# Turning q, k and the exponentials by transposing transfers instead of on TensorE

## The chip, the cores and the metric

The kernel runs on one core of one Trainium2 chip. The metric is the device time of one execution in microseconds. In the profile PE is TensorE (matmuls), PEld its weight loads, DVE is VectorE, ACT is ScalarE, POOL is GpSimd (here it issues loads), SP is SyncE (here it issues transfers within SBUF, and stores).

## The reference

Attention with a few global tokens, then a two-layer network over all tokens:

```python
batch, n_heads, seq_l, seq_g, head_dim = (8, 8, 512, 32, 64)      # window = 32
out_g = matmul(softmax(q_g @ [k_g, k_l].T * scale), [v_g, v_l])   # 32 global queries see all 544 keys
s_ll = where(|pos_q - pos_k| <= 32, q_l @ k_l.T * scale, -1e9)    # 512 local queries see a band
out_l = matmul(softmax([q_l @ k_g.T * scale, s_ll]), [v_g, v_l])  # and the 32 global keys
x = concat([out_g, out_l]).transpose(0, 2, 1, 3).reshape(4352, 512)
h = x @ w_in                                                      # 512 -> 2048
out = (h * clip(h + 3, 0, 6) / 6) @ w_out                         # 2048 -> 512, float32
```

## The kernel before

Work is cut into operations, each with an engine, a length, the operations it depends on, the buffer that it takes and those that it gives back, and a key (when it should come). `Plan.lay` (from line 98) lays them out ahead of time: at each step it takes the operation that can start first, by lengths and latencies written into the kernel, and of those that start within 40 ns the one with the lowest key. For transfers it keeps a small model of two queues, POOL's and SP's (`Transfers`, line 27). The result is a fixed order for every engine and queue; on the chip each engine goes through its order and waits for semaphores where its next instruction isn't ready. Attention of a batch is meant to run `AHEAD` keys (line 470) before the network of that batch; a batch's network is 4 keys long. Where PE would be idle before batch 2, filler matmuls on a tile of zeros are put in (line 944).

For each batch b of 8:

- Loads (POOL, line 380): four tiles of 128 rows of q and k go to `nat` (4 buffers, float16, q and k side by side: 128 x 2 x 512), v to `ve`. q and k of the global tokens go to `natg`.
- `turn_qk` (line 547): eight matmuls with the identity (line 556) turn one `nat` tile, 128x128 each, into the PSUM tile `t`, of which there is one; one copy on ACT or DVE (lines 284, 286) moves it to `qk`, where the head's 64 dimensions lie on partitions and the rows along the free side. `turn_g` (line 568) does the same for the global rows. `qk` has two buffers, by b % 2.
- Strips: from batch 1 on, seven transfers on SP's queue (line 519) put copies of `ve` into `st` so that each 32 queries find their 96 local rows of v and the 32 global ones on 128 partitions.
- `local_step` (line 595), four times per batch: scores `s` of 128 queries for 8 heads (lines 614, 621, 628), then for each head the masked smallest value of the negated scores (DVE, line 640) and the exponential with its sum (ACT, line 651), then the division by the sum into `pn` (two DVE instructions, line 665, four heads each). Eight matmuls with the identity (line 672) turn `pn` (128 queries x 8 heads x 128 keys) into `t`; a copy moves it to `et`. The product with the strips (`av`, lines 690 and 695) goes to `a`, and two copies put it into `xt`, the network's input.
- `global_steps` (line 720) does the 32 global queries, with turnings of its own (line 766) and the product at line 780.
- `moe_local` (line 842): the first layer (line 802) in 16 groups of four 128x512 matmuls, a relu on ACT (line 809) and the combining product on DVE (line 813) into `gs`; the second layer (line 824) in 16 groups of four, for four tiles of 128 rows; a copy to `ot` and a store on SP's queue (line 839). After all batches `moe_global` does the same for the 256 global rows.

`pn` and `et` have two buffers each (lines 257 and 258), `sm`, which feeds `pn`, has two, and `t` is shared by all turnings.

Of the kernel before, what the change touches and what calls it, by code (L numbers as in the profile page):

```python
# [9 lines left out]
FP16 = mybir.dt.float16  # L10
# [63 lines left out]
class Plan:  # L74
# [5 lines left out]
    AHEAD, WAIT = 0.3, 0.0  # L80
# [7 lines left out]
    def add(self, eng, dur, emit, deps=(), key=0.0, acq=None, rel=(), dma=None):  # L88

        o = Op(eng, dur, emit, deps, key, acq, rel, 0, dma)  # L90
        o.can = {eng: dur} if isinstance(eng, str) else dict(zip(eng, dur))
        o.n = len(self.ops)
        self.ops.append(o)
        for r in rel:
            r.held += 1
        return o
# [101 lines left out]
def kernel(  # L198
# [12 lines left out]
    nc = tc.nc  # L211
    P = 128

    B, H, Sl, D = q_l.shape
# [3 lines left out]
    NP = H // 2  # L218
    NJ = Sl // P
    NDFF = dff // P  # L220
    G = Sg
    UQ = 32
    NU = P // UQ
    KL = 3 * UQ
    KC = Sl + 2 * UQ
# [14 lines left out]
    def many(n, shape, dtype, name, pool=sb):  # L240
        return [pool.tile(shape, dtype, tag=f"{name}{i}", name=f"{name}{i}") for i in range(n)]

    NS, NX = 2, 3
    psS = many(1, [P, 2, 512], FP32, "s", pp)
    psT = many(1, [P, 1024], FP16, "t", pp)
    psA = many(1, [P, 2, 512], FP32, "a", pp)
    psM = many(3, [P, 512], FP32, "m", pp)

    nat = many(4, [P, 2, HD], FP16, "nat")
    natg = many(2, [P, HD], FP16, "natg")  # L250
    gt = many(2, [P, NP, P], FP16, "gt")
    kgz = many(2, [P, NP, 2, G], FP16, "kgz")
    qk = many(2, [P, NP, 2, KC], FP16, "qk")
    ve = many(2, [P, NV, HD], FP16, "ve")
    st = many(2, [P, NJ * NU, HD], FP16, "st")
    sm = many(NS, [P, H, P], FP32, "sm")
    pn = many(NS, [P, H, P], FP16, "pn")
    et = many(2, [P, H, P], FP16, "et")
    sg = many(2, [P, S], FP32, "sg")
    pg = many(2, [P, NV * P], FP16, "pg")  # L260
    eg = many(1, [P, 2, NV, P], FP16, "eg")
# [16 lines left out]
    add = plan.add  # L278
# [3 lines left out]
    def copy(op, out, in_):  # L282
        if op.eng == "ACT":
            nc.scalar.copy(out=out, in_=in_)  # L284
        else:
            nc.vector.tensor_copy(out=out, in_=in_)  # L286
# [65 lines left out]
    def clear():  # L352
        for r in range(2):
            for p in range(NP):
                nc.vector.memset(qk[r][:, p, 1, 0:UQ], 0.0)
                nc.vector.memset(qk[r][:, p, 1, KC - UQ:KC], 0.0)
            nc.vector.memset(ve[r][:, NJ, :], 0.0)
        nc.vector.memset(kgz[1], 0.0)

# [67 lines left out]
    def turn_first(na, lq, lk, nh, lh):  # L427

        def pe_q(op):
            ps = psM[op.slot].bitcast(FP16)  # L430
            for p in range(NP):
                nc.tensor.matmul(out=ps[:, p * P:(p + 1) * P], lhsT=nat[na.slot][:, 0, p * P:(p + 1) * P],
                                 rhs=ident, is_transpose=True)
        tq = add("PE", 225, pe_q, [na, lq, prep["ident"]], key=-5.5, acq="M", rel=[na])

        def ev_q(op):
            copy(op, qk[0][:, :, 0, UQ:UQ + P], psM[tq.slot].bitcast(FP16)[:, 0:NP * P].rearrange(
                "d (p s) -> d p s", p=NP))
        q = add(BOTH, (450, 300), ev_q, [tq, prep["clear"]], key=-7.5, rel=[tq])
        w = P + UQ  # L440

        def pe_k(op):
            ps = psM[op.slot].bitcast(FP16)
            for p in range(NP):
                nc.tensor.matmul(out=ps[:, p * w:p * w + P], lhsT=nat[na.slot][:, 1, p * P:(p + 1) * P],
                                 rhs=ident, is_transpose=True)
                nc.tensor.matmul(out=ps[:, p * w + P:(p + 1) * w],
                                 lhsT=pn[nh.slot].rearrange("s h d -> s (h d)")[0:UQ, p * P:(p + 1) * P],
                                 rhs=ident[0:UQ, 0:UQ], is_transpose=True)
        tk = add("PE", 350, pe_k, [na, lk, lh, prep["ident"]], key=-5.5, acq="M", rel=[na, nh])  # L450

        def ev_k(op):
            copy(op, qk[0][:, :, 1, UQ:UQ + w], psM[tk.slot].bitcast(FP16)[:, 0:NP * w].rearrange(
                "d (p s) -> d p s", p=NP))
        return q, add(BOTH, (540, 380), ev_k, [tk, prep["clear"]], key=-7.5, rel=[tk])

# [10 lines left out]
        return o  # L467

    gav = {}
    TIGHT, AHEAD, KEPT, PART, W_OUT = 2, 6.0, 1, {0: 128, 1: 256}, -5.5  # L470
    BLOCKS = ((0, 1), (2, 3))
    SPREAD = 0

# [70 lines left out]

    def turn_qk(b, j, ld, key, which=(0, 1)):
        r = b % 2
        w0, n = which[0], len(which)

        def pe(op):
            ps = psT[op.slot]
            for i in which:
                for p in range(NP):
                    c0 = ((i - w0) * NP + p) * P
                    nc.tensor.matmul(out=ps[:, c0:c0 + P], lhsT=nat[ld[0].slot][:, i, p * P:(p + 1) * P],  # L556
                                     rhs=ident, is_transpose=True)
        t = add("PE", 225 * n, pe, [*ld, prep["ident"]], key=key, acq="T", rel=ld[:1])

        def ev(op):  # L560
            copy(op, qk[r][:, :, w0:w0 + n, UQ + j * P:UQ + (j + 1) * P],
                 psT[t.slot][:, 0:n * NP * P].rearrange("d (i p s) -> d p i s", i=n, p=NP))
        deps = [t, prep["clear"]]
        if b >= 2:
            deps += [S_op[b - 2, jj] for jj in range(max(j - 1, 0), min(j + 1, NJ - 1) + 1)] + gS_op[b - 2]
        return add(BOTH, (450 * n, 300 * n), ev, deps, key=key - 2, rel=[t])

    def turn_g(b, ld, key, after=()):
# [26 lines left out]
    def local_step(b, j, key):  # L595
# [9 lines left out]
        def pe(op):  # L605
            ps = psS[op.slot]
            if kept:
                for p in range(NP):
                    for u in range(NU):
                        q0 = UQ + j * P + u * UQ  # L610
                        for lo, n, at in pieces(u) + [(None, G, place_g(u))]:
                            for e in range(2):
                                rows = slice(e * D, (e + 1) * D)
                                nc.tensor.matmul(out=ps[u * UQ:(u + 1) * UQ, e, p * P + at:p * P + at + n],
                                                 lhsT=qk[r][rows, p, 0, q0:q0 + UQ],
                                                 rhs=gt[g][rows, p, kg0:kg0 + G] if lo is None
                                                 else qk[r][rows, p, 1, q0 - UQ + lo:q0 - UQ + lo + n])
                return
            for p in range(NP):
                for e in range(2):  # L620
                    nc.tensor.matmul(out=ps[:, e, p * P:p * P + G],
                                     lhsT=qk[r][:, p, 0, UQ + j * P:UQ + (j + 1) * P], rhs=kgz[r][:, p, e, :])
            for p in range(NP):
                for u in range(NU):
                    for e in range(2):
                        rows = slice(e * D, (e + 1) * D)
                        q0 = UQ + j * P + u * UQ
                        nc.tensor.matmul(out=ps[u * UQ:(u + 1) * UQ, e, p * P + G:(p + 1) * P],  # L628
                                         lhsT=qk[r][rows, p, 0, q0:q0 + UQ],
                                         rhs=qk[r][rows, p, 1, q0 - UQ:q0 + 2 * UQ])  # L630
        s = add("PE", 900 if kept else 600, pe, [qkT[b, j], keyT[b, j], keyT[b, 0 if b == j == 0 else min(j + 1, NJ - 1)], kg[b]], key=key, acq="S")
        S_op[b, j] = s
        first = None
# [36 lines left out]
        def tr(op):  # L670
            for h in range(H):
                nc.tensor.matmul(out=psT[op.slot][:, h * P:(h + 1) * P], lhsT=pn[pn_op.slot][:, h, :],  # L672
                                 rhs=ident, is_transpose=True)
        t = add("PE", 450, tr, scs, key=key - 0.2, acq="T", rel=[pn_op])
        et_op = add("DVE", 0, lambda op: None, [t], key=key - 0.3, acq="et")

        def ev(op):
            copy(op, et[et_op.slot].rearrange("k h q -> k (h q)"), psT[t.slot])
        e_ = add(BOTH, (900, 600), ev, [et_op], key=key - 2, rel=[t])

        tight = b < TIGHT

# [37 lines left out]
    def global_steps(b, key):  # L720
# [5 lines left out]
        for e in range(2):  # L726
            rows = slice(e * D, (e + 1) * D)

            def pe(op, rows=rows):
                ps = psS[op.slot].rearrange("q a c -> q (a c)")  # L730
                for p in range(NP):
                    nc.tensor.matmul(out=ps[p * G:(p + 1) * G, 512 - G:512], lhsT=gt[g][rows, p, g0:g0 + G],
                                     rhs=gt[g][rows, p, g0 + G:g0 + 2 * G])
                for p in range(NP):
                    nc.tensor.matmul(out=ps[p * G:(p + 1) * G, 512:1024], lhsT=gt[g][rows, p, g0:g0 + G],
                                     rhs=qk[r][rows, p, 1, UQ:UQ + Sl])
            s = add("PE", 360, pe, [gT[b // 2]] + [keyT[b, j] for j in range(NJ)], key=key + 0.2 * e, acq="S")
            gS_op[b].append(s)
            so = add("DVE", 0, lambda op: None, [s], key=key, acq="stat")
# [32 lines left out]
            def ev(op, e=e, t=t):  # L772
                copy(op, eg[eg_op.slot][:, e].rearrange("k i q -> k (i q)"), psT[t.slot][:, 0:NV * P])
# [208 lines left out]
```

## Time and profile before

| | |
|---|---|
| median of 3 runs | 356.17 us (355.71 to 357.87) |
| the profiled execution | 355.24 us |
| its span, first to last instruction | 353.5 us |
| its granted TensorE clock, mean | 0.995 |
| turning q and k (L556), matmuls | 248, 31 groups of 8 |
| turning exponentials (L672), matmuls | 256, 32 groups of 8 |
| copies of 128x1024 out of `t`, to `qk` | 18 on DVE (683 ns), 13 on ACT (1021 ns) |
| the same to `et` | 18 on DVE (687 ns), 14 on ACT (1009 ns) |

Times on an engine are those of the profiled execution. The mean time of one matmul is longer than what it takes of PE, since matmuls follow each other in a pipeline; what a group takes is read from its start to the start of the next group.

### The profile page before, as it was taken

Reading aid. Unit: us, or ns where it says so; the run is one execution under the profiler, and the core shown is the slowest. Engines: PE = TensorE matmul, PEld = TensorE weight load, DVE = VectorE, ACT = ScalarE, POOL = GpSimd, SP = SyncE. Lnnn points to the kernel's source line nnn. Section 1 sums busy time; section 2 is a strip of 40 time slices with the busy share of each in tenths; the row PEclk is TensorE's granted clock in tenths of the full one; section 3 lists DMA queues with packets and bytes.
Section 4 is the critical chain, followed back from the end, with each engine's and each line's share of the span. In section 5 each row is a group of like instructions: output and inputs, shape, how many; then the busy total and the mean of one; then the engine's idle time right before and its main releaser. Section 6 shows DMA issues by size and latency. Waiting matters only on the chain.

```text
span 353.5 us, 11319 instructions
## 1 busy us (share of the span) xinstructions
PE 339.5 (96%) x4414; PEld 204.0 (58%) x4414; DVE 279.5 (79%) x1004; ACT 258.8 (73%) x792; POOL 106.2 (30%) x139
## 2 busy tenths in 40 slices
PE   7977979999999999999999999999999999999995
PEld 3565877667965555555555555555465544445642
DVE  6999978989996999888998899886997794076300
ACT  3898859759885999587987799859976893275411
POOL 8929712931680514151525123500000000000000
PEclk9999989999999999999999999999999999999999
DMA  9999999999999999599998999795001100200012
GB/s 158 174 195 131 172 253 164 138 189 259 91 149 240 168 219 103 37 154 179 166 64 123 193 159 70 68 212 146 0 32 41 53 2 0 91 30 1 32 51 98
DMA packets 123093, 42.47 MB, mean 120 GB/s; under 512 B 108320, under 2 KB 116000, under 8 KB 123040
## 3 DMA queue, kind: packets, MB, share of 16 engines
q0 software_dynamic: 106560, 17.05, 65.2%
q1 hardware_dynamic: 16480, 24.71, 24.9%
q8 instruction: 34, 0.56, 0.6%
q14 instruction: 19, 0.16, 0.1%
HBM read 35.19 MB, written 8.91 MB: 125 GB/s over the span
## 4 chain that ended last, share of the span: by engine, by line
PE 56%; DVE 20%; DMA 11%; POOL 7%; issue 3%; ACT 1%; SPq 0%; POOLq 0%; ACTq 0%
PE m L824 27%; PE m L802 18%; DVE gs L813 7%; DMA wout<-in_moe_w_out_dram 6%; DVE sm L640 4%; DMA win<-in_moe_w_in_dram 3%; POOL ve L380 3%; DVE pn L665 3%; POOL nat L380 2%; PE a L695 2%; PE t L672 2%; PE t L556 2%; PE s L628 2%; DVE xt L286 1%; DMA ve<-in_v_l_dram 1%
## 5 line engine op out<-in xcount | busy, mean ns | idle before, releaser
L824 PE MATMUL m<-wout,gs 128*128 128x512 f16 x544 | 130.3, 379 | 0.1
L802 PE MATMUL m<-xt,win 128*128 128x512 f16 (+2 forms) x768 | 124.7, 312 | 0.7 <-DVE gs L813 0.6
L813 DVE SCALAR_TENSOR_TENSOR gs<-t,m 128x512 f16<-128x512 f32 x136 | 91.2, 681 | 30.3 <-ACT t L809 29.7
L651 ACT ACTIVATE sm<-sm,stat 128x128 f32<-128x128 f32 x256 | 100.0, 394 | 16.1 <-DVE stat L640 15.7
L809 ACT ACTIVATE t<-m 128x512 f32<-128x512 f32 x136 | 81.1, 599 | 25.5 <-PE m L802 24.2
L802 PEld LDWEIGHTS <-win 128*128 128x128 f16 x832 | 70.1, 100 | 47.0 <-issue 5.3
L824 PEld LDWEIGHTS <-gs 128*128 128x128 f16 x544 | 49.7, 98 | 49.7 <-issue 1.0
L640 DVE CUSTOM_DVE_ANT_0 sm<-s,mask 128x128 f32<-128x128 f32 x256 | 59.8, 283 | 5.3 <-PE s L628 4.6
L651 ACT ACTIVATION_READ_ACCUMULATOR sm<-sm,stat 128x1 f32 x256 | 49.1, 192 | 0.0
L380 POOL DMA_DIRECT2D nat<-in_q_l_dram x30 | 27.1, 902 | 67.2 <-PE t L556 60.8
L665 DVE TENSOR_TENSOR pn<-sm,stat 128x512 f16<-128x512 f32 x64 | 43.9, 686 | 0.7
L284 ACT COPY ot<-m 128x512 f32<-128x512 f32 x24 | 14.1, 586 | 28.8 <-PE m L824 25.9
L380 POOL DMA_DIRECT2D ve<-in_v_l_dram x40 | 32.1, 821 | 0.2
L380 POOL DMA_DIRECT2D nat<-in_k_l_dram x30 | 27.2, 907 | 4.3 <-DVE stat L640 3.0
L284 ACT CAST xt<-a 64x512 f16<-64x512 f32 (+1 forms) x35 | 20.2, 577 | 7.1 <-PE a L695 4.7
L640 DVE DVE_READ_ACCUMULATOR2_ANT stat<- 128x1 f32 x256 | 21.1, 83 | 0.0
L672 PEld LDWEIGHTS <-pn 128*128 128x128 f16 x256 | 16.7, 98 | 6.7 <-issue 0.7
L556 PE MATMUL t<-ident,nat 128*128 128x128 f16 x248 | 19.1, 219 | 1.2 <-DVE qk L286 0.9
L556 PEld LDWEIGHTS <-nat 128*128 128x128 f16 x248 | 15.9, 98 | 6.9 <-issue 2.1
L672 PE MATMUL t<-ident,pn 128*128 128x128 f16 x256 | 19.7, 219 | 0.1
L944 PE MATMUL a<-idle 128*128 128x512 f16 x54 | 16.0, 420 | 3.6 <-DVE xt L286 1.8
L695 PEld LDWEIGHTS <-st 128*128 128x128 f16 x384 | 14.1, 98 | 4.2
(81 smaller groups left out, 318.3 us busy)
## 6 DMA issues: line engine op xcount, KB each, us to landing
out_dram<-ot SPq DMA_DIRECT2D x32, 256.0 KB, 3.5
st<-ve SPq DMA_DIRECT2D x14, 384.0 KB, 5.3
nat<-in_q_l_dram POOLq DMA_DIRECT2D x30, 128.0 KB, 4.8
nat<-in_k_l_dram POOLq DMA_DIRECT2D x30, 128.0 KB, 5.3
st<-ve SPq DMA_DIRECT2D x7, 512.0 KB, 7.1
st<-ve SPq DMA_DIRECT2D x14, 256.0 KB, 6.1
ve<-in_v_l_dram POOLq DMA_DIRECT2D x24, 128.0 KB, 5.5
win<-in_moe_w_in_dram POOLq DMA_DIRECT2D x4, 512.0 KB, 9.6
```

The lines of the kernel that those rows point to most:

```text
L284: nc.scalar.copy(out=out, in_=in_)
L380: nc.gpsimd.dma_start(out=dst(op), in_=src)
L556: nc.tensor.matmul(out=ps[:, c0:c0 + P], lhsT=nat[ld[0].slot][:, i, p * P:(p + 1) * P], rhs=ident, is_transpose=True)
L640: nc.vector.tensor_tensor_reduce(out=sm[sm_op.slot][:, h, :], in0=psS[s.slot][:, e, p * P:(p + 1) * P], in1=m, scale=-scale, scalar=3.0e38 ...
L651: nc.scalar.activation(out=sm[sm_op.slot][:, h, :], in_=sm[sm_op.slot][:, h, :], func=EXP, scale=-1.0, bias=stat[stat_op.slot][:, 0, h:h + 1],
L665: (nc.gpsimd if op.eng == "POOL" else nc.vector).tensor_tensor(out=pn[pn_op.slot][:, h0:h1, :], in0=sm[sm_op.slot][:, h0:h1, :], in1=stat[ ...
L672: nc.tensor.matmul(out=psT[op.slot][:, h * P:(h + 1) * P], lhsT=pn[pn_op.slot][:, h, :], rhs=ident, is_transpose=True)
L695: nc.tensor.matmul(out=ps[:, p // 2, c0:c0 + 64], lhsT=st[r][:, u * NJ + j, p * P:(p + 1) * P], rhs=et[et_op.slot][:, 2 * p:2 * p + 2, u * ...
L802: nc.tensor.matmul(out=psM[op.slot][:, i * n:(i + 1) * n], lhsT=w_in_t[:, m, (c + i) * P:(c + i + 1) * P], rhs=x()[:, m, t0:t0 + n], start ...
L809: nc.scalar.activation(out=t1[to.slot], in_=psM[f.slot], func=RELU, bias=0.5, scale=1.0 / 6.0)
L813: nc.vector.scalar_tensor_tensor(out=gs[set_.slot][:, c:c + k, t0:t0 + n], in0=t1[to.slot].rearrange("f (k t) -> f k t", k=k), scalar=1.0, ...
L824: nc.tensor.matmul(out=psM[(f or op).slot], lhsT=gs[set_.slot][:, c, t0:t0 + P], rhs=w_out_t[:, c, :], start=(c == 0), stop=(c == NDFF - 1))
```

## The change

For batches 2 to 7, q and k are turned by a transposing transfer on SP's queue, straight from `nat` to `qk`; for batches 3 to 7, so are the exponentials, from `pn` to `et`. Each moves 128 x 1024 float16 values, 256 KB. The eight matmuls, their use of `t` and the copy go for these steps. `qk` changes the order of its middle dimensions, so that one transfer writes q and k of a tile. `pn` and `et` get a third buffer, `AHEAD` goes from 6 to 5. The planner takes a turning transfer as 1250 ns of SP's queue and 64 packets.

```diff
-    qk = many(2, [P, NP, 2, KC], FP16, "qk")
+    qk = many(2, [P, 2, NP, KC], FP16, "qk")
...
-    pn = many(NS, [P, H, P], FP16, "pn")
-    et = many(2, [P, H, P], FP16, "et")
+    pn = many(3, [P, H, P], FP16, "pn")
+    et = many(3, [P, H, P], FP16, "et")
...
-    TIGHT, AHEAD, KEPT, PART, W_OUT = 2, 6.0, 1, {0: 128, 1: 256}, -5.5
+    TIGHT, AHEAD, KEPT, PART, W_OUT = 2, 5.0, 1, {0: 128, 1: 256}, -5.5
...
+    def old_qk(b, j):
+
+        if b < 2:
+            return []
+        return [S_op[b - 2, jj] for jj in range(max(j - 1, 0), min(j + 1, NJ - 1) + 1)] + gS_op[b - 2]
+
+    TURN_QK, TURN_E, TURN = 2, 3, (64, 225.0)
+
     def turn_qk(b, j, ld, key, which=(0, 1)):
         r = b % 2
+        if b >= TURN_QK:
+            def move(op):
+                nc.sync.dma_start_transpose(out=qk[r][:, :, :, UQ + j * P:UQ + (j + 1) * P].rearrange(
+                    "d i p s -> d (i p) s"), in_=nat[ld[0].slot].rearrange("s i c -> s (i c)"))
+            return add("SP", 1250, move, [*ld, prep["clear"], *old_qk(b, j)], key=key, rel=ld[:1], dma=TURN)
...
-        t = add("PE", 450, tr, scs, key=key - 0.2, acq="T", rel=[pn_op])
-        et_op = add("DVE", 0, lambda op: None, [t], key=key - 0.3, acq="et")
-
-        def ev(op):
-            copy(op, et[et_op.slot].rearrange("k h q -> k (h q)"), psT[t.slot])
-        e_ = add(BOTH, (900, 600), ev, [et_op], key=key - 2, rel=[t])
+        if b < TURN_E:
+            t = add("PE", 450, tr, scs, key=key - 0.2, acq="T", rel=[pn_op])
+            et_op = add("DVE", 0, lambda op: None, [t], key=key - 0.3, acq="et")
+
+            def ev(op):
+                copy(op, et[et_op.slot].rearrange("k h q -> k (h q)"), psT[t.slot])
+            e_ = add(BOTH, (900, 600), ev, [et_op], key=key - 2, rel=[t])
+        else:
+            def move(op):
+                nc.sync.dma_start_transpose(out=et[op.slot], in_=pn[pn_op.slot].rearrange("q h k -> q (h k)"))
+            e_ = et_op = add("SP", 1250, move, scs, key=key - 2, acq="et", rel=[pn_op], dma=TURN)
```

In the new file the scores stand at lines 625, 632 and 639, the turning of exponentials on PE at 683, their transfer at 694, the transfer of q and k at 559, the products at 706 and 711, the network's layers at 818 and 840.

More of the change, by code (lines that the diff above doesn't have):

```diff
@@ L354, in clear @@
             for p in range(NP):
-                nc.vector.memset(qk[r][:, p, 1, 0:UQ], 0.0)
-                nc.vector.memset(qk[r][:, p, 1, KC - UQ:KC], 0.0)
+                nc.vector.memset(qk[r][:, 1, p, 0:UQ], 0.0)
+                nc.vector.memset(qk[r][:, 1, p, KC - UQ:KC], 0.0)
             nc.vector.memset(ve[r][:, NJ, :], 0.0)
@@ L436, in ev_q @@
         def ev_q(op):
-            copy(op, qk[0][:, :, 0, UQ:UQ + P], psM[tq.slot].bitcast(FP16)[:, 0:NP * P].rearrange(
+            copy(op, qk[0][:, 0, :, UQ:UQ + P], psM[tq.slot].bitcast(FP16)[:, 0:NP * P].rearrange(
                 "d (p s) -> d p s", p=NP))
@@ L452, in ev_k @@
         def ev_k(op):
-            copy(op, qk[0][:, :, 1, UQ:UQ + w], psM[tk.slot].bitcast(FP16)[:, 0:NP * w].rearrange(
+            copy(op, qk[0][:, 1, :, UQ:UQ + w], psM[tk.slot].bitcast(FP16)[:, 0:NP * w].rearrange(
                 "d (p s) -> d p s", p=NP))
@@ L560, in ev @@
         def ev(op):
[L561 to L565, printed above, removed]
+            copy(op, qk[r][:, w0:w0 + n, :, UQ + j * P:UQ + (j + 1) * P],
+                 psT[t.slot][:, 0:n * NP * P].rearrange("d (i p s) -> d i p s", i=n, p=NP))
+        deps = [t, prep["clear"]] + old_qk(b, j)
         return add(BOTH, (450 * n, 300 * n), ev, deps, key=key - 2, rel=[t])
@@ L614, in pe @@
                                 nc.tensor.matmul(out=ps[u * UQ:(u + 1) * UQ, e, p * P + at:p * P + at + n],
-                                                 lhsT=qk[r][rows, p, 0, q0:q0 + UQ],
+                                                 lhsT=qk[r][rows, 0, p, q0:q0 + UQ],
                                                  rhs=gt[g][rows, p, kg0:kg0 + G] if lo is None
-                                                 else qk[r][rows, p, 1, q0 - UQ + lo:q0 - UQ + lo + n])
+                                                 else qk[r][rows, 1, p, q0 - UQ + lo:q0 - UQ + lo + n])
                 return
@@ L621, in pe @@
                     nc.tensor.matmul(out=ps[:, e, p * P:p * P + G],
-                                     lhsT=qk[r][:, p, 0, UQ + j * P:UQ + (j + 1) * P], rhs=kgz[r][:, p, e, :])
+                                     lhsT=qk[r][:, 0, p, UQ + j * P:UQ + (j + 1) * P], rhs=kgz[r][:, p, e, :])
             for p in range(NP):
@@ L628, in pe @@
                         nc.tensor.matmul(out=ps[u * UQ:(u + 1) * UQ, e, p * P + G:(p + 1) * P],
-                                         lhsT=qk[r][rows, p, 0, q0:q0 + UQ],
-                                         rhs=qk[r][rows, p, 1, q0 - UQ:q0 + 2 * UQ])
+                                         lhsT=qk[r][rows, 0, p, q0:q0 + UQ],
+                                         rhs=qk[r][rows, 1, p, q0 - UQ:q0 + 2 * UQ])
         s = add("PE", 900 if kept else 600, pe, [qkT[b, j], keyT[b, j], keyT[b, 0 if b == j == 0 else min(j + 1, NJ - 1)], kg[b]], key=key, acq="S")
@@ L735, in pe @@
                     nc.tensor.matmul(out=ps[p * G:(p + 1) * G, 512:1024], lhsT=gt[g][rows, p, g0:g0 + G],
-                                     rhs=qk[r][rows, p, 1, UQ:UQ + Sl])
+                                     rhs=qk[r][rows, 1, p, UQ:UQ + Sl])
             s = add("PE", 360, pe, [gT[b // 2]] + [keyT[b, j] for j in range(NJ)], key=key + 0.2 * e, acq="S")
```

## The prediction

> **What bounds the kernel now.** I read the page from the top: busy shares first, then the chain that ended last, then the busy time by stage, then the matmuls in order of time, and last the transfers with their times to landing.
>
> ```profile
> span 353.5 us, 11319 instructions
> ...
> PE 339.5 (96%) x4414; PEld 204.0 (58%) x4414; DVE 279.5 (79%) x1004; ACT 258.8 (73%) x792; POOL 106.2 (30%) x139
> ...
> DMA  9999999999999999599998999795001100200012
> ```
>
> PE has 14 us without work in the whole span; DVE and ACT have 74 and 95. The busy time by stage (columns: stretch, its length, PE, PEld, DVE, ACT, POOL, granted clock, DMA share, GB/s) says where those 14 us lie:
>
> ```profile
> 0.00:60.00 60.00, 51.19 (x1078) 37.74 (x1079) 52.47 (x219) 45.55 (x144) 35.20 (x51) 0.97 1.55 181
> ...
> 134.00:165.00 31.00, 31.00 (x378) 17.36 (x375) 27.60 (x100) 24.75 (x83) 11.57 (x14) 1.00 0.92 102
> 165.00:200.00 35.00, 34.92 (x454) 20.11 (x453) 32.87 (x121) 28.21 (x92) 13.36 (x18) 1.00 1.05 138
> 200.00:240.00 40.00, 39.84 (x479) 22.32 (x478) 34.14 (x121) 33.70 (x103) 10.36 (x13) 1.00 1.01 139
> ```
>
> 8.8 us of them come before 60 us, where the change does nothing, and 3.75 after the last matmul. From 134 us to the end PE is never without work, at a granted clock of 1.00. So from there on a microsecond of PE work that goes is a microsecond of span, unless a wait takes its place. The matmuls in order of time show what one turning costs:
>
> ```profile
> 226.56 0.61 PE L672 MATMUL t<-ident,pn 128*128 128x128 f16 x8
> 227.01 1.89 PE L824 MATMUL m<-wout,gs 128*128 128x512 f16 x8
> 228.74 0.63 PE L695 MATMUL a<-et,st 128*128 128x64 f16 x16
> 229.20 1.89 PE L824 MATMUL m<-wout,gs 128*128 128x512 f16 x8
> ...
> 235.03 0.61 PE L556 MATMUL t<-ident,nat 128*128 128x128 f16 x8
> 235.47 1.03 PE L824 MATMUL m<-wout,gs 128*128 128x512 f16 x4
> ```
>
> A turning of eight blocks holds PE from its start to the next group's start: 0.45 us (226.56 to 227.01) and 0.44 us (235.03 to 235.47), not the 0.61 of its row, which runs into the next group. In the same way a four-matmul group of L802 or L824 holds it 0.87 us, the scores of a step (L621 and L628) 0.58, the attention product (L695) 0.46, the global scores 0.36, one global turning 0.28, the global product 0.58.
>
> The transfers that are nearest to a turning one (KB of each, median us from issue to landing):
>
> ```profile
> out_dram<-ot SPq DMA_DIRECT2D x32, 256.0 KB, 3.5
> ...
> st<-ve SPq DMA_DIRECT2D x7, 512.0 KB, 7.1
> st<-ve SPq DMA_DIRECT2D x14, 256.0 KB, 6.1
> ```
>
> **The change, part by part.** *PE.* q and k: six batches of four tiles are 24 turnings; exponentials: five batches of four steps are 20. 44 x 0.447 = 19.7 us of PE work go. Nothing comes in: the other groups are the same in number, but for one filler matmul less. All of it lies after 60 us, where PE is full, so all of it is on the path: -19.7.
>
> *DVE and ACT.* 44 evictions of 128x1024 go (683 to 687 ns on DVE, 1009 to 1021 on ACT), and the planner spreads the rest anew. By the new order DVE loses 10 of et, 12 of qk, 2 of ot, 4 of xt and 2 of gt and gains 3 of eg: 18.5 us. ACT loses 10 of et, 12 of qk, 3 of eg and gains 2 of ot and 5 of xt: 20 us. Neither bounds the stages above, so I count nothing. The cover is PE's full queue; if PE began to wait for evictions this would be a gain, not a loss.
>
> *SP's queue.* It held 94 transfers and now holds 138. The trace shows no turning transfer. Its time from issue to landing is bounded below by the store of the same 256 KB, 2.6 us in the stage from 134 to 165, and above, for a transfer that behaves like others on this queue, by the 512 KB broadcast's 7.1. The strips of 256 KB go out in trains of seven behind each other, so 6.1 holds some queueing; the last of one train, with the loads done, took 3.9. I take 5.0: one transfer of 256 KB from SBUF to SBUF, like that lone strip, but beside the loads. The queue is served in order, and 15 of the 44 turnings stand straight behind a store, which waits for an eviction of MoE output. Those evictions belong to groups that PE runs earlier than the product that needs the turning. I take nothing for it and allow 2 us in the range. Each turning transfer also waits for the transfer eight places back to land; at 138 transfers in 350 us that is 20 us back.
>
> *What PE now waits for.* Before, a step of attention ran scores, smallest values (L640), exponentials (L651), scaling (L665), turning on PE, eviction, product. In the trace the first steps of batches 4 to 7 need 5.1 to 5.6 us from the end of the scores to the end of the second scaling (258.54 to 263.66 in batch 7, 183.67 to 189.03 in batch 5), and then 2.2 us to the product (226.56 to 228.74). Now the transfer stands in those 2.2 us. With 5.4 + 5.0 and 0.1 for the start, a product can start 10.5 us after its scores. I added up the PE work that the new order puts between them, from the group times above. In batch 7's first step: four groups of L824 that make 0.87 + 1.73 + 0.87 + 0.87, three of L802 at 0.87, two scores at 0.58 and the global product 0.58, in all 8.7 us. The other short ones: steps (4,0) 10.6, (5,0) 9.8, (5,3) 11.0, (6,0) 9.8, (6,2) 12.3, (7,0) 8.7, (7,3) 12.7; batch 3 has 14.9 to 20. The steps left out have more, or already hold an earlier step's wait in between. PE's queue is in order, so what falls short is a stall of everything behind it: at 10.5 it is 0.7 + 0.7 + 1.8 = 3.2 us. At 9.0 it is 0.3; at 12 it is 1.4 + 2.2 + 1.0 + 2.2 + 3.3 = 10.1; at 13.5 it is 19.6, and the gain is gone. So the point that decides is a landing 8.0 us after the scaling.
>
> *q and k.* In the new order of SP's queue the transfers of a batch from 4 on stand ahead of exponentials of the batch before it, which are ready 20 to 31 us of PE work ahead of that batch's scores. A landing of 7.1 costs nothing there. Batch 2's are nearer, in a stage (60 to 100 us) where strips and stores took 7 to 8 us to land; 0 to 2 us, taken as 0 since the loads of that batch wait for buffers, not the other way.
>
> *Three buffers, and attention less ahead.* The third pn and et buffers hold what a transfer keeps longer. AHEAD 5 moves loads and scores later against the MoE matmuls; at the end 16 instead of 48 second-layer matmuls stand between the last global product and batch 7's first layer: the same work in another place, 0. It costs if batch 7's attention is late, since 32 x 0.2165 = 6.9 us of cover have gone from there; that is in the sums above, by step (7,0) and (7,3).
>
> *The transfer engines.* 44 x 256 KB = 11.3 MB on top of 42.5. The DMA line shows slices at 9 or more up to 240 us, but the rate inside them goes from 37 to 259 GB/s, so a busy slice is not a full one; at 231 to 350 GB/s (strips alone, after 240 us) a batch's eight turnings are some 6 to 9 us of a batch's 36. That is an estimate. There is room, and it is the reason to take 5.0 and not 3.9.
>
> *Sum.* The profiled execution took 355.24 us, of which 353.5 are span. 355.24 - 19.7 + 3.2 = 338.7. The median of the runs is 0.93 above that execution, so 339.7.
>
> **A rule against the change.** A matmul turning of 128x128 takes 0.447/8 = 0.056 us of PE here, with an eviction of 0.69 or 1.0 us for eight of them on engines that have time. The Trainium skill, "VectorE: DVE Perf Modes", section "The three transpose paths", gives TensorE 390 ns and the DMA crossbar 1309 ns for one 128x128 tile. For TensorE the trace disagrees by seven times, as matmuls follow each other. For the transfer no run here shows it; eight tiles in a row at that figure would be an estimate of 10.5 us, and the sum 375 (38.5 us come back) in place of 339.7.
>
> **Rivals.** *No wait at all* (landing up to 3.5, as the store's median): 19.7 less and 0 to 0.3 back, 336.5. For it: the stores in quiet stages. Against: a turning transfer takes its bytes apart, and loads run beside it.
>
> *Contested transfers*: landings of 6.5 to 8 us, as strips and stores between 60 and 100 us. At 12 to 13.5 us from scores to product 10 to 19.6 come back: 346.6 to 356. For it: the loads of the next batch run at the same time. Against: from 134 us on the stores took 2.6 to 4.2.
>
> *Slower: the blocks of a turning go one after another.* If one transfer takes as long as the slowest strip in the trace, 11.2 us, a product follows its scores by 5.4 + 11.2 = 16.6 us. By the same list of distances 44 us come back (7.9 in step (7,0), 6.8 each in (5,0) and (6,0), 5.6 in (5,3), 4.3 each in (4,0) and (6,2), 3.9 in (7,3), 4.3 in four others): 356.17 - 19.7 + 44 = 380. It decides from 8.0 us on. The rule of the Trainium skill above comes out near this. For it: nothing in the trace shows such a transfer. Against: all transfers of this size on this queue land in under 8 us at the median.
>
> **How the numbers follow.** Forecast 0.48 (landing 3.5 to 6.5: 336.5 to 346), no wait 0.14, contested 0.18, slower 0.20. The range leaves out part of the last and the best: 335 to 360. Within 1% (352.6 to 359.7) is about what a measurement of this kernel can't tell from no change. Two thirds of the contested case end under 352.6: faster 0.48 + 0.14 + 0.12 = 0.74; same 0.06; slower 0.20.
>
> **What would show it.** Right: PE busy near 320 us, full from 134 us on, DVE near 260, ACT near 238; turning transfers landing in about 5 us; idle time of PE ahead of L711 (the product) of some 3 us, most of it in the first steps of batches 5 to 7. Wrong: landings above 8 us, idle PE ahead of L711 of 20 us or more; or idle PE ahead of the scores (L632, L639), which I put at nothing: q and k late, held behind a store on SP's queue or behind a load.

## The result, and the profile after

The changed kernel is slower: its time is 1.038 of the time before, 95% interval 1.027 to 1.048 (median 373.72 us of 4 runs against 357.02). The medians in this document take in a few runs in which the granted clock was lower by some per cent; the ratios leave those out. The profiled execution took 368.84 us, its span is 367.1, against 353.5 before; I take the difference of 13.6 us apart with it.

The busy shares and the slices of the profile after:

```profile
span 367.1 us, 10660 instructions
...
PE 328.6 (90%) x4061; PEld 186.5 (51%) x4061; DVE 264.4 (72%) x978; ACT 242.9 (66%) x774; POOL 106.0 (29%) x139
...
PEclk9989999999999989898989999999999999999998
DMA  9999999999999999999992999999813312110013
```

PE is without work for 38.5 us instead of 14.0, and the granted clock has dips between 128 and 193 us that were not there before. By stage (stretch, length, PE, PEld, DVE, ACT, POOL, granted clock, DMA share, GB/s):

```profile
134.00:165.00 31.00, 26.15 (x300) 13.46 (x298) 20.07 (x82) 19.14 (x67) 8.55 (x11) 0.91 1.46 196
165.00:200.00 35.00, 26.86 (x245) 12.70 (x243) 19.61 (x66) 19.48 (x57) 8.83 (x12) 0.90 1.35 166
200.00:240.00 40.00, 34.11 (x400) 17.43 (x397) 31.38 (x117) 28.42 (x96) 11.57 (x14) 1.00 1.39 176
```

These stages had almost no idle PE before (0.2 us in all three); now they have 4.9, 8.1 and 5.9 us, two of them at a clock of 0.9. The waits name what ended it (us in total, times, longest):

```profile
POOL nat L380 <- DMA qk<-nat: 69.0, 8, 20.5
...
PE a L711 <- DMA et<-pn: 19.5, 7, 3.6
...
PE t L583 <- DMA natg<-in_k_g_dram: 4.8, 1, 4.8
```

The products waited seven times for the exponentials' transfers, 19.5 us, and one turning of global rows waited 4.8 us for its load: together 24.3 of the 24.5 us of added idle time. The first line is POOL: a load of q and k waits until the transfer of the tile that held its buffer has landed. Before, the loads waited for PE's turnings in the same way:

```profile
POOL nat L380 <- PE t L556: 60.8, 13, 10.3
```

The sum is hardly larger now, but the longest single wait is twice as long. (The expectations below speak of 23 us ahead of the products; that sum counted one wait twice, on PE and on its weight loads.)

The transfers (KB each, where the page has it, and median us to landing):

```profile
out_dram<-ot SPq DMA_DIRECT2D x32, 256.0 KB, 3.2
st<-ve SPq DMA_DIRECT2D x14, 384.0 KB, 8.5
nat<-in_q_l_dram POOLq DMA_DIRECT2D x30, 128.0 KB, 7.6
nat<-in_k_l_dram POOLq DMA_DIRECT2D x30, 128.0 KB, 9.5
...
qk<-nat SPq DMA_TRANSPOSE x24, 6.7
et<-pn SPq DMA_TRANSPOSE x20, 7.5
```

Turnings take 6.7 and 7.5 us at the median, and the transfers beside them became slower as well: loads of q from 4.8 to 7.6, of k from 5.3 to 9.5 us. But a turning that nothing runs beside is quick. The transfers of the stretch from 301.9 to 305.1 us, with one turning and nothing else:

```profile
DMA packets 1056, 0.26 MB, mean 82 GB/s; under 512 B 1056, under 2 KB 1056, under 8 KB 1056
...
q1 hardware_dynamic: 1056, 0.26, 42.5%
...
et<-pn SPq DMA_TRANSPOSE x1, 3.0
```

It lands in 3.0 us, goes in 1056 packets, not in the planner's 64, and holds the 16 engines for 42.5% of 3.2 us, 1.36 us. The stretch from 130 to 134 us, with loads of q and k and a broadcast beside:

```profile
nat<-in_k_l_dram POOLq DMA_DIRECT2D x2, 128.0 KB, 11.8
nat<-in_q_l_dram POOLq DMA_DIRECT2D x1, 128.0 KB, 13.0
qk<-nat SPq DMA_TRANSPOSE x1, 10.7
et<-pn SPq DMA_TRANSPOSE x1, 12.4
```

The same transfer takes 12.4 us there.

A landing counts from the issue, and some transfers stood on SP's queue before that. The queue's rows (start, and time that the issue took):

```profile
117.97 4.39 SPq L559 DMA_TRANSPOSE qk<-nat  x1
122.48 3.67 SPq L694 DMA_TRANSPOSE et<-pn  x1
126.26 0.54 SPq L855 DMA_DIRECT2D out_dram<-ot  x1
129.44 0.67 SPq L519 DMA_DIRECT2D st<-ve  x1
130.23 1.31 SPq L559 DMA_TRANSPOSE qk<-nat  x1
131.63 7.09 SPq L694 DMA_TRANSPOSE et<-pn  x1
138.81 0.53 SPq L855 DMA_DIRECT2D out_dram<-ot  x1
139.53 2.58 SPq L519 DMA_DIRECT2D st<-ve  x4
142.21 2.24 SPq L694 DMA_TRANSPOSE et<-pn  x1
```

The three transfers of `et` are those of batch 3's first three steps. Their scalings (L676) ended at 117.7, 122.3 and 134.6 us, so they stood 4.8, 9.3 and 7.6 us, behind issues of up to 7.09 us, where the shortest issue of a turning takes 1.23, and behind a strip that waited for its load. Their products waited 3.60, 2.34 and 2.51 us, which is 8.5 of the 19.5. Issued at once and with the same landings (9.5, 12.4 and 11.3 us) all three would have been there before PE ran out of work, at 128.4, 141.7 and 151.0 us; that is an estimate. The other four waits, 11.0 us, are those of steps (4,0), (5,0), (5,2) and (6,0), whose transfers went out within 0.1 us of their scalings and landed after 7.3 to 10.8 us.

What a wait costs beyond itself, from PE's matmuls in order of time:

```profile
132.04 0.65 PE L711 MATMUL a<-et,st 128*128 128x64 f16 x16 [3.60 <-DMA et<-pn]
132.53 3.19 PE L818 MATMUL m<-xt,win 128*128 128x512 f16 x8
135.51 0.42 PE L632 MATMUL s<-kgz,qk 128*128 128x32 f16 x8
```

After 3.60 us without work eight matmuls take 2.98 us (132.53 to 135.51) in place of 1.73: the granted clock of the stretch from 132 to 136 us is 0.62. The clock fell after four of the eight waits for transfers, those of 3.60, 2.51, 3.34 and 4.80 us, and stayed at 1.00 after those of 2.34, 2.87, 2.46 and 2.37. Three of the stretches that follow a wait (columns as above):

```profile
132.00:136.00 4.00, 3.96 (x48) 2.03 (x55) 1.56 (x3) 2.34 (x6) 0.11 (x1) 0.62 1.89 214
153.50:156.00 2.50, 2.47 (x62) 2.08 (x62) 0.62 (x5) 1.39 (x3) 0.00 (x0) 0.50 1.56 131
216.50:219.00 2.50, 2.48 (x25) 1.45 (x25) 0.82 (x2) 1.33 (x3) 0.39 (x1) 1.00 1.95 216
```

So three things stand against the 19.7 us that went: 19.5 us of waits at products, 4.8 at a global turning, and 8.8 us by which PE's busy time (328.6) is above the 339.5 - 19.7 = 319.8 that its work took before. 355.24 - 19.7 + 19.5 + 4.8 + 8.8 = 368.6, and 368.84 was measured. This sum has to come out, since the span is PE's busy and idle time; what it tells is how the loss divides. Of the 8.8 us the clock accounts for some 6: in windows of 2 us, busy time times the missing share of the clock adds up to 7.8 us, against 1.7 in the kernel before (an estimate). The rest stays open.

### The profile page after: what moved, and what is told of

The parts are those of the page before. It is cut to its first block, busy times and chain, and to the rows that moved or that the text cites. A ratio compares the mean times of both kernels' runs of the same rounds, so it can differ in the third digit from the quotient of the medians.

```text
span 367.1 us, 10660 instructions
## 1 busy us (share of the span) xinstructions
PE 328.6 (90%) x4061; PEld 186.5 (51%) x4061; DVE 264.4 (72%) x978; ACT 242.9 (66%) x774; POOL 106.0 (29%) x139
## 3 DMA queue, kind: packets, MB, share of 16 engines
q0 software_dynamic: 106560, 17.05, 64.7%
## 4 chain that ended last, share of the span: by engine, by line
PE 55%; DMA 22%; DVE 17%; issue 2%; ACT 2%; SPq 1%; POOL 0%; ACTq 0%; POOLq 0%
PE m L840 23%; PE m L818 18%; DMA et<-pn 13%; DVE gs L829 5%; DVE sm L651 4%; DMA natg<-in_k_g_dram 4%; DVE pn L676 3%; PE a L711 3%; DMA ve<-in_v_l_dram 2%; PE a L960 2%; PE s L639 1%; DVE st L286 1%; DMA qk<-nat 1%; DMA t<-in_k_l_dram 1%; PE t L683 1%
## 5 line engine op out<-in xcount | busy, mean ns | idle before, releaser
L662 ACT ACTIVATE sm<-sm,stat 128x128 f32<-128x128 f32 x256 | 100.2, 395 | 14.9 <-DVE stat L651 13.8
L818 PEld LDWEIGHTS <-win 128*128 128x128 f16 x832 | 71.0, 100 | 52.1 <-issue 8.1
L651 DVE CUSTOM_DVE_ANT_0 sm<-s,mask 128x128 f32<-128x128 f32 x256 | 61.6, 283 | 8.6 <-PE s L639 7.2
L676 DVE TENSOR_TENSOR pn<-sm,stat 128x512 f16<-128x512 f32 x64 | 43.9, 686 | 0.8
L284 ACT CAST xt<-a 64x512 f16<-64x512 f32 (+1 forms) x39 | 22.6, 579 | 28.6 <-PE a L711 20.3
L711 PE MATMUL a<-et,st 128*128 128x64 f16 x384 | 15.9, 195 | 19.5 <-DMA et<-pn 19.5
L284 ACT COPY ot<-m 128x512 f32<-128x512 f32 x26 | 15.2, 585 | 26.3 <-PE m L840 23.3
L380 POOL DMA_DIRECT2D nat<-in_k_l_dram x30 | 26.7, 890 | 10.7 <-DMA nat<-in_k_l_dram 6.0
L711 PEld LDWEIGHTS <-st 128*128 128x128 f16 x384 | 15.0, 99 | 26.1 <-issue 17.7
L960 PE MATMUL a<-idle 128*128 128x512 f16 x53 | 18.1, 474 | 3.4 <-DVE xt L286 1.8
L286 DVE CAST xt<-a 64x512 f16<-64x512 f32 (+1 forms) x17 | 11.7, 686 | 10.4 <-ACT xt L284 5.2
L768 ACT ACTIVATE sg<-s,stat 128x544 f32<-128x544 f32 x16 | 11.4, 715 | 10.8 <-DVE stat L762 8.8
L672 DVE RECIPROCAL stat<-stat 128x4 f32<-128x4 f32 x64 | 11.0, 172 | 5.9 <-ACT sm L662 5.2
```

The lines of the kernel that those rows point to most:

```text
L380: nc.gpsimd.dma_start(out=dst(op), in_=src)
L651: nc.vector.tensor_tensor_reduce(out=sm[sm_op.slot][:, h, :], in0=psS[s.slot][:, e, p * P:(p + 1) * P], in1=m, scale=-scale, scalar=3.0e38 ...
L662: nc.scalar.activation(out=sm[sm_op.slot][:, h, :], in_=sm[sm_op.slot][:, h, :], func=EXP, scale=-1.0, bias=stat[stat_op.slot][:, 0, h:h + 1],
L676: (nc.gpsimd if op.eng == "POOL" else nc.vector).tensor_tensor(out=pn[pn_op.slot][:, h0:h1, :], in0=sm[sm_op.slot][:, h0:h1, :], in1=stat[ ...
L711: nc.tensor.matmul(out=ps[:, p // 2, c0:c0 + 64], lhsT=st[r][:, u * NJ + j, p * P:(p + 1) * P], rhs=et[et_op.slot][:, 2 * p:2 * p + 2, u * ...
L818: nc.tensor.matmul(out=psM[op.slot][:, i * n:(i + 1) * n], lhsT=w_in_t[:, m, (c + i) * P:(c + i + 1) * P], rhs=x()[:, m, t0:t0 + n], start ...
```

## The experiments

Theory A: turnings and loads share the transfer engines, which slows both; products wait, and the clock falls after the waits. Rival B: the exponentials' turnings are late because of where they stand in SP's queue. Rival C: the other parts of the change (less ahead, third buffers, the new order in `qk`) cost the time.

### Parts of the change

```diff
-    TURN_QK, TURN_E, TURN = 2, 3, (64, 225.0)
+    TURN_QK, TURN_E, TURN = 2, 8, (64, 225.0)
```

> Only q and k are turned by transfers (24 of the 44); exponentials go back to PE. Ratio to the kernel before. Theory A (turning transfers and loads slow each other down, and PE waits for the exponentials' transfers): the 24 x 0.447 = 10.7 us of PE work go, no product waits for a transfer, q and k stand 20 us and more ahead of their scores, so 343 to 349 us. Theory B (turnings of exponentials stand behind other transfers on SP's queue): the same, since none is left there. Theory C (less attention ahead, or the third buffers, cost the time): 355 or more, since these parts stay. A loses if PE waits here for q and k or for strips by more than 5 us.

Measured: ratio 1.003 (0.999 to 1.007), median 358.55 us. The 343 to 349 us of A and B are missed. The time alone is in C's range (355 or more), but the run without any turning, below, takes C away. PE waits for no exponentials, and still the 10.7 us are gone. One place has them:

```profile
164.63 1.99 PE L818 MATMUL m<-xt,win 128*128 128x512 f16 x8
176.09 0.59 PE L583 MATMUL t<-ident,natg 128*128 128x128 f16 x4 [9.46 <-DMA natg<-in_k_g_dram]
176.47 5.15 PE L818 MATMUL m<-xt,win 128*128 128x512 f16 x12
```

A wait of 9.46 us for the loads of global rows, and after it twelve matmuls that take 5.0 us (to the next group at 181.45) in place of 2.6. 9.5 + 2.4 is more than the gain. These loads stand on POOL's queue behind loads of q and k that waited for a buffer (6.2 and 9.1 us, from 139 to 156 us), and the buffer comes free only when a turning transfer has landed. That is a second path from the slow transfers to PE, which A as I had put it did not have; it is tested further below.

`TURN_QK, TURN_E = 8, 3`:

> Only exponentials are turned by transfers (20 of the 44); q and k go back to PE. 20 x 0.447 = 8.9 us of PE work go. Theory A: less than half of the added transfer time is left, so landings fall from 7.5 us at the median to some 5, idle PE ahead of the products from 23 us to 5 to 12, and the time is 350 to 358 us. Theory B: q and k no longer stand in between on SP's queue, but strips and stores do: landings counted from the issue stay at 7 or more, idle PE ahead of the products stays above 15 us, 362 or more. Theory C: 360 or more with little idle PE ahead of the products.

Measured: ratio 1.019 (1.013 to 1.026), median 364.62 us. Landings of the exponentials' turnings fall to 4.8 us at the median, the products wait 12.8 us. The landings are A's (5 us) and the waits just above A's range. The time is above A's range and in B's (362 or more), but B's landings of 7 us and waits of 15 are not there, and no transfer of exponentials stood on SP's queue for more than 1.8 us after its scaling. The time is above A's because the products' waits, 12.8 us, and a busy time of PE that is 3.5 us longer than 339.5 - 8.9 come to more than the 8.9 us of work that went.

`TURN_QK, TURN_E = 8, 8`:

> No turning by transfers: only the new order of qk's dimensions, the third pn and et buffers and attention 5 keys ahead. Theories A and B: within 2% of the kernel before, 352 to 363 us. Theory C: 365 or more, most of what the whole change lost.

Measured: ratio 1.000 (0.997 to 1.004). C falls.

### Taking the loads away

```diff
-            o.append(load(lambda op, i=i: rows(nat[(o[0] if i else op).slot][:, i, :]),
-                          heads(src[b, :, j * P:(j + 1) * P, :]), P * H,
+            o.append(load(lambda op, i=i: rows(nat[(o[0] if i else op).slot][0:(P if b < 3 else 16), i, :]),
+                          heads(src[b, :, j * P:j * P + (P if b < 3 else 16), :]), P * H,
...
-        o.append(load(lambda op: rows(ve[r][p0:p1, i, :]), heads(v_l[b, :, s0 + p0:s0 + p1, :]), (p1 - p0) * H,
+        o.append(load(lambda op: rows(ve[r][p0:(p1 if b < 3 else p0 + 16), i, :]), heads(v_l[b, :, s0 + p0:s0 + (p1 if b < 3 else p0 + 16), :]), (p1 - p0) * H,
```

> The whole change, every engine's order as it stands; but from batch 3 on a load of q, k or v moves 16 rows instead of up to 128, so an eighth of the packets (the rest of the tile keeps an earlier batch's rows; the numbers that come out are not the reference's). Theory A: turning transfers land in 3 to 5 us, idle PE ahead of the products falls from 23 us below 5, the granted clock is back at 0.99, 338 to 346 us. Theory B: the order on SP's queue is the same, so landings counted from the scaling stay long, idle PE stays above 15 us, 360 or more. Theory C: 355 or more with little idle PE ahead of the products.

Measured: ratio 0.951 (0.945 to 0.958), median 338.32 us. The planner's lengths and packet counts are untouched, so the order is that of the changed kernel; only the loads from batch 3 on move less. Its profile:

```profile
PE 320.5 (96%) x4061; PEld 184.4 (55%) x4061; DVE 262.1 (78%) x978; ACT 241.1 (72%) x774; POOL 84.2 (25%) x139
```
```profile
PE a L711 <- DMA et<-pn: 0.3, 1, 0.3
```
```profile
qk<-nat SPq DMA_TRANSPOSE x24, 5.0
...
et<-pn SPq DMA_TRANSPOSE x20, 3.7
```

PE's work is 320.5 us, the 319.8 of the sum; the exponentials land in 3.7 us, the products wait 0.3 us in all, and the kernel takes what was forecast for the change. This is A: the loads beside the turnings make them slow. SP's order, unchanged, costs nothing by itself: no transfer of exponentials stood on the queue for more than 1.8 us after its scaling, against 9.3 in the changed kernel. So B's place, 8.5 us of the waits there, is a further effect of A: where issues are slow, what stands behind them is late too. Which of the things that loads and turnings share makes them slow, no run here separates.

### The second path: loads behind late buffers

Loads of global rows one key earlier, with q and k alone (`TURN_E = 8`), then with the whole change:

```diff
-                        lg[b // 2].append(load_g(b, i, k, base + (1.5 + 0.1 * i + 0.05 * k) * stepk,
+                        lg[b // 2].append(load_g(b, i, k, base - 1.0 + (1.5 + 0.1 * i + 0.05 * k) * stepk,
```

> Only q and k turned by transfers, and the loads of the global rows one key earlier, so that POOL issues them ahead of the q and k loads that wait for a buffer until its transfer has read it. Theory A, with POOL's queue as its second place: the run with q and k alone lost its gain in one stall of 9.5 us (a global turning waiting for its load) and the lower clock after it; with that load early the stall goes, and 24 x 0.447 = 10.7 us come through: 344 to 350 us. Rival (slower loads and strips cost the same time anywhere): another wait of 5 us or more takes its place, 354 to 360.

Measured: ratio 0.971 (0.965 to 0.977), median 348.28 us. The wait is gone and 10.4 us of the 10.7 come through, though loads of q now land only after 11.8 us at the median and POOL still waits:

```profile
POOL nat L380 <- DMA qk<-nat: 50.0, 8, 16.6
```

These waits are hidden; 9.5 of them at one load were not. This kernel beats both, by changing two numbers of the changed one. Early global loads without any turning by transfers were not run; PE had no wait for these loads in the kernel before, so they had none to take off there.

> The whole change with the loads of the global rows one key earlier. If POOL's queue behind late buffers is a cause of its own: the 4.8 us wait of a global turning goes, and some 2 to 3 us of lower clock with it, 361 to 367 us; idle PE ahead of the products stays near 20 us. If it is not: 368 or more.

Open in time: four runs took 362.18 to 371.43 us, and they give no ratio. In the profile, of a run of 368.04 us, no global turning waits, and the products wait 23.3 us in place of 19.5: most of the wait did not come off, it stands at the products.

### Telling the planner

`TURN = (1056, 32.0)` in place of `(64, 225.0)`, which makes a transfer 2.1 us of all engines to the planner instead of 0.9:

> The whole change, but the planner takes a turning transfer as 1056 packets of 32 ns (what the trace of the changed kernel shows for one) in place of 64 of 225 ns, so its order leaves more PE work between scores and product. Theory A1 (the transfers are slow and the order leaves too little distance for that): idle PE ahead of the products falls from 23 us to under 8, 350 to 360 us. Theory A2 (the transfer engines are full between 60 and 250 us, no order helps): the waits move to loads, strips or scores, 362 or more.

Measured: ratio 1.008 (1.004 to 1.012), median 360.22 us, at the upper edge of A1's range. No product waits for a transfer now, but PE does elsewhere:

```profile
PE s L632 <- DVE stat L651: 6.1, 4, 2.6
PE t L583 <- DMA natg<-in_k_g_dram: 5.7, 1, 5.7
PE m L818 <- DVE gs L829: 3.8, 9, 0.7
PE s L748 <- ACT sg L768: 2.4, 1, 2.4
```

Scores wait for the one score buffer, since the order bunches them. So the planner's number was worth 3 points of the 3.8 (A1), but most of the gain doesn't come back (A2). The order of SP's queue changed with it: transfers of exponentials now go out at most 2.7 us after their scalings. Whether the longer distance on PE or the shorter stand on the queue gave the 3 points, this run doesn't separate.

Both repairs, `TURN` and the early global loads:

> The whole change with both repairs: the planner takes a turning transfer as 1056 packets of 32 ns, and the loads of the global rows come one key earlier. With the order told alone no product waited for a transfer, but a global turning waited 5.7 us for its load and scores waited some 10 us for buffers where the order bunches them. If each repair takes its own wait: 345 to 354 us, ratio 0.965 to 0.99. If the full transfer engines only move the wait: ratio 1.00 or more, with a new wait of 5 us or more.

Measured: ratio 1.014 (1.012 to 1.016). The wait at the global turning is gone and the time isn't: the repairs don't add up. PE is idle for 31.0 us of its span of 358.2, in many places; the largest, 6.0 us in two waits, is scores that wait for the score buffer.

> q and k alone by transfers, the early global loads, and the planner's transfer of 1056 packets of 32 ns. PE had nothing left to wait for in that run without the last part, so both theories give the same: ratio 0.96 to 0.975, unless the later scores that the order now allows for cost a wait, then 0.98 or more.

Measured: ratio 0.990 (0.986 to 0.994); the planner's better number makes the order worse here than the wrong one did (0.971). Why, the waits don't show: none is over 3.1 us. Of the 6.0 us by which its profiled span is longer (349.5 against 343.5), 4.2 are busy time of PE, on 3 matmuls more. That stays open.

### Is it the turning, the bytes, or the pieces?

All 44 as plain copies of the same 256 KB, in the same places:

```diff
-                nc.sync.dma_start_transpose(out=qk[r][:, :, :, UQ + j * P:UQ + (j + 1) * P].rearrange(
-                    "d i p s -> d (i p) s"), in_=nat[ld[0].slot].rearrange("s i c -> s (i c)"))
+                nc.sync.dma_start(out=qk[r][:, :, :, UQ + j * P:UQ + (j + 1) * P].rearrange(
+                    "d i p s -> d (i p) s"), in_=nat[ld[0].slot].rearrange("s i (p c) -> s (i p) c", p=NP))
...
-                nc.sync.dma_start_transpose(out=et[op.slot], in_=pn[pn_op.slot].rearrange("q h k -> q (h k)"))
+                nc.sync.dma_start(out=et[op.slot], in_=pn[pn_op.slot])
```

> The whole change, same order, but each turning transfer is a plain copy of the same 256 KB between the same tiles (q and k in 1024 pieces of 256 B, exponentials in 128 of 2 KB), so nothing is turned and the output is not the reference's. Theory T (a turning transfer takes more of the transfer engines than a copy of its size): landings of the exponentials' copies fall to 3 to 5 us, idle PE ahead of the products below 8 us, 340 to 352 us. Theory S (any 44 transfers of 256 KB in these places on SP's queue cost this): landings stay at 7 us, 362 or more.

Measured: ratio 0.970 (0.965 to 0.975). T holds: the same bytes, places and order, and 6.8 points less than with turnings. The exponentials' copies land in 5.1 us at the median, just above T's 3 to 5, and the products wait 6.9 us.

With rows of `et` padded, so that the exponentials' copies go in pieces of 256 B too (`et = [t[:, :, 0:P] for t in many(3, [P, H, P + 16], FP16, "et")]`):

> As the run with plain copies, but the exponentials' copies also go in 1024 pieces of 256 B (rows of et padded by 16 values), so all 44 have a turning transfer's number of packets and bytes and nothing is turned; the output is not the reference's. Theory P (the number of small packets is what costs): idle PE ahead of the products comes back to 15 us or more, ratio 1.02 or more. Theory X (the turning itself costs): ratio 0.965 to 0.985, as with the larger pieces.

Measured: ratio 0.996 (0.991 to 1.000). Neither forecast: it lies between. Of the 6.8 points from plain copies to turnings, 2.6 come with the small pieces and 4.2 with the turning. The queue's engine time says the same: SP's queue took 24.9% of 353.5 us before, which is 88 us, and 180 (turned), 153 (small pieces), 140 us (large pieces of exponentials) after, so (180 - 88) / 44 = 2.1, 1.5 and 1.2 us for one transfer. That is an estimate, which takes the queue's other transfers as unchanged. With the small loads it still gives 1.9 for a turning; what went there is the loads' own time, from 64.7% of 367.1 us to 37.3% of 334.3. Whether the rest is the turning itself or SP's issue of it, 1.23 us at the least where a copy in small pieces takes 0.59, and up to 7.1 us beside loads, no run here separates.

### Exponentials only where the loads are over

`TURN_QK, TURN_E = 2, 6`, with the early global loads:

> q and k turned by transfers from batch 2 on, exponentials only for batches 6 and 7, the loads of the global rows one key earlier: 32 of the 44 transfers. Theory A (a turning transfer is late because of the loads beside it): when batches 6 and 7 are scored the loads are over (in the run with q and k and early global loads they end near 225 us), so these eight transfers land in 3 to 4 us, no product waits over 2 us in all, and 8 x 0.447 = 3.6 us more come off than in that run: ratio 0.955 to 0.965. If the exponentials' transfers are late wherever they stand: idle PE ahead of the products of 5 us or more, ratio 0.975 or more.

Measured: ratio 0.969 (0.959 to 0.979). The eight turnings land in 3.5 us at the median, as A has it; one took 6.4, and the products wait 2.5 us in all, half a microsecond more than A's bound. The 3.6 us are not to be seen: the interval reaches into A's range (up to 0.965) and into the other's (0.975 and more), and the ratio without them, 0.971, lies in the middle. So the landings and the waits speak for A; the time doesn't decide.

## Why the prediction was wrong

*19.7 us of PE work.* Right: 320.5 us of busy time where nothing waits.

*DVE and ACT.* About right in size (264.4 and 242.9, forecast near 260 and 238), and they bound nothing.

*The landing, "I take 5.0".* This is the step that failed. The rows that bounded it, 2.6 to 7.1 us, are of transfers in few large packets. Alone a turning is faster than I took (3.0); beside loads it is slower than the upper end: 7.5 at the median over all, 7.3 to 12.4 in the seven steps that waited.

*"There is room" in the transfer engines.* Wrong, and it is why the landing was: I took a batch's eight turnings as 6 to 9 us of its 36, from the rate of strips. By the estimate above they are 8 x 2.1 = 17 us. The page could have warned: strips and stores took 7 to 8 us to land between 60 and 100 us; from 63 us on that stage's DMA share was 1.58, and the change makes the later stages like that (1.46 and 1.35, from 0.92 and 1.05).

*SP's queue, "I take nothing for it".* This failed too. I asked which transfers stand behind a store that waits, and not how long an issue takes. Three transfers stood 4.8 to 9.3 us behind slow issues, and 8.5 of the 19.5 us of waits hang on that, more than the 2 us that I allowed.

*The distances in PE's order.* They held where they can be read: PE ran out of work 9.8 us after the scores of step (5,0) and 9.9 after those of (6,0), where the list has 9.8 for both. But at 5.4 + 7.5 + 0.1 = 13.0 us from scores to product the list gives 16 us, and that this is near the measured 19.5 is luck. Of its seven short steps only (4,0), (5,0) and (6,0) waited, 8.6 us. Steps (5,3), (6,2), (7,0) and (7,3) did not, (7,0) with the shortest distance of all, since their turnings landed in 3.1 to 3.4 us. Batch 3, which the list had at 14.9 us and more, waited 8.5, and step (5,2) 2.5.

*q and k cost nothing.* Their scores did not wait, but I followed only who reads `qk` and not who waits for `nat`: the loads behind, and the global loads behind those. 4.8 us here, 9.5 with q and k alone.

*The clock.* Not in the sum: some 6 of the 8.8 us by which PE's busy time is longer. Each wait was priced at its own length.

*The rivals.* "Contested transfers", given 0.18, was the mechanism; at the measured waits it gives 355.0, and the two missing terms make it 368.6. "Blocks one after another" is refuted: a lone turning lands in 3.0 us, and the estimate from the Trainium skill, "VectorE: DVE Perf Modes", section "The three transpose paths", was 10.5. That the result is slower was that rival's sign, not its reason. That contested transfers are the reason is shown by the run with small loads, not by the sum.

## What to carry to other kernels

Price a transfer that takes the place of engine work beside the transfers that will run with it, by the number of its packets and the engine time that it adds, not by a lone transfer of its bytes; and ask for each buffer that it reads who waits to fill it again. Move first what is needed late: q and k, 20 us ahead of their use, gave 3% once a queue behind them was put right, while the exponentials, which in the short steps are needed some 3 to 7 us after they are ready, cost more than they saved (1.019 by themselves). When a planned order misses, a wait on PE can cost more than its length, because the clock may fall after it: here it did after four of eight waits. And a slow transfer makes late what stands behind it on its queue, so look at the time of an issue as well as at the landing.

## What was not expected of the hardware

- A turning of 128x1024 float16 values by a transfer is 1056 packets; alone it lands in 3.0 to 3.1 us and runs at some 210 GB/s, beside loads it takes up to 13.4 us to land and some 2.1 us of all 16 engines, by the estimate above. The Trainium skill, "Advanced Engine Details and Errata", section "X-Bar Transpose (TRN2)", says that transposing transfers are as fast as regular ones. Alone, the least landings agree (3.0, against 2.9 for a copy in pieces of 256 B; in pieces of 2 KB it is 2.2); in this kernel the times do not: 1.038 against 0.996.
- A wait of 2.51 us on PE was followed by a granted clock of 0.50 over the next 2.5 us (153.5 to 156.0), while after one of 2.87 it stayed at 1.00. The first came 7 us after another wait of 2.34 us; whether that matters, no run here shows. The Trainium skill, "TensorE: Matmul & The Clock Gate", section "Why this matters for your kernels", sets the bound at gaps of about 3 us; the waits of 3.34, 3.60 and 4.80 us agree with it, the one of 2.51 does not.
